# Ten TensorE transposes of an attention and MLP kernel given to the DMA queue, and spatial weights loaded later

## Chip, cores and metric

The kernel runs on one core of a Trainium2 chip. The metric is device time in microseconds (us) of one execution. Before the change the median of three runs is 210.61 us (210.47 to 212.0).

## What is computed

Block-sparse attention over 4 batches of 8 heads, 768 positions, head width 64, and after it a gated MLP with a spatial (position by position) product. Cut to what matters:

```python
scores = q @ k.T / sqrt(D)                   # mask: band, edges, sampled blocks of 32
attn   = exp(scores - max) ; attn /= attn.sum(-1)
x      = (attn @ v), heads side by side      # (4, 768, 512)
h      = relu(x @ w_in)                      # (4, 768, 1024)
u, v   = h[..., :512], h[..., 512:]
v_n    = (v - mean(v)) / sqrt(var(v) + 1e-6)
v_s    = w_spatial @ v_n + b_spatial         # over positions
out    = (u * v_s) @ w_out
```

## The kernel before

**Pairs.** Two heads make a pair; pairs 0 to 3 are batch 0, pairs 4 to 15 the other three. For a pair, q, k and v are loaded as float32 (`st_q`, `st_k`, `st_v`, 384 KB each, `load`, L105) by the SP queue and cast to bfloat16 by GpSimd (`cast`, L117): q and k into `nat`, v into `vv`. TensorE needs q and k with the head dimension on the partitions, in the tile `kq`. For pairs 1 to 3 TensorE transposes them through PSUM and VectorE copies them out (`tr_first`: k and the first third of q; `tr_rest`, L346: the last two thirds of q). From pair 4 on one DMA transpose does a whole pair (`tr_dma`, L365: `nat` to `tt`), and VectorE copies each head out of `tt` into `kq` (`split`, L369).

**Slots.** The work is written out by hand as a list of slots, one after another. Slot s issues the score matmuls of step s into one of two PSUM tiles (tag `sc`), from which ScalarE takes the exponential into `a_all`, then the attention-times-v matmuls (AV) of an earlier step, then whatever `when(slot, ...)` put there, then as many matmuls of the MLP as a pace gives (`run_queue`), and at last what stands in `late[slot]`. Each engine runs its own instructions in this order; an instruction that waits holds all behind it on its engine, and this holds for SP, which issues nearly all DMAs.

**The first 36 slots** are batch 0, in which the mask is applied, so that it goes by units of one third of the queries: `UNITS` (L377) are head 0 and head 1 of pair 0 (two thirds of the queries), then pairs 1, 2, 3 with the first third (units 2, 3, 4), pairs 1, 2, 3 with the second (units 5, 6, 7), and pairs 0 to 3 with the last (units 8 to 11). A unit takes three slots: unit u scores in slots 3u to 3u + 2, and its AV matmuls follow three slots later. So the last third of q of pair 1, 2 and 3 is first wanted in slots 27, 30 and 33. Slot 36 is the first with the unmasked `qk_full` of pair 4, head 0 of `kq`.

**From attention to the MLP.** When a unit's AV is done, VectorE normalizes it into `xn` (L431; tiles `xn3`, three buffers), and `xtr_third` (L491) has TensorE transpose it into the unused end of its own PSUM tile and VectorE copy it into `xt`, one tile per pair, of which the unit fills its third. The MLP of batch 0 runs in steps of one matmul: product v2 (and v3, u2, u3) is dealt out from slot 29 on, and its four matmuls load as weights, in turn, the second third of `xt` of pairs 0, 1, 2, 3. The product's result is taken out of PSUM by VectorE (`vn`, `un`).

**Spatial weights.** `w_spatial` comes in six loads of 384 KB (`ws_load`, L517), each cast by GpSimd in three pieces (`ws_cast`, L522), and each two are transposed by one DMA (`ws_tr`, L530) into `w_spt`, which the spatial products of batch 0 use first.

Of the kernel before, what the change touches and what calls it, by code (L numbers as in the profile page):

```python
# [11 lines left out]
BF16 = mybir.dt.bfloat16  # L12
# [14 lines left out]
def kernel(  # L27
# [16 lines left out]
    nc = tc.nc  # L44

    B, H, S, D = q.shape
# [3 lines left out]
    NCH = S // 128  # L50
# [6 lines left out]
    NG = H // 2  # L57
# [4 lines left out]
    NT = 3  # L62
    TC = NCH // NT
    TW = TC * 128
# [4 lines left out]
    const = ctx.enter_context(tc.tile_pool(name="const", bufs=1))  # L69
# [12 lines left out]
    kq = const.tile([128, H, 2 * S], BF16, name="kq")  # L82
# [6 lines left out]
    def qcols(t0, n=1):  # L89
        return slice(S + t0 * TW, S + (t0 + n) * TW)  # L90
# [20 lines left out]
    nat = {}  # L111
# [97 lines left out]
    def dve_copy(o, i):  # L209
        nc.vector.tensor_copy(out=o, in_=i)  # L210
# [47 lines left out]
    def bank(nm="ps", tag=None):  # L258
        return psum.tile([128, 1024], BF16, tag=tag or moe_tag(), bufs=2 if tag else 1, name=nm)

    def tr(ps, c, in_):
        nc.tensor.transpose(out=ps[:, c * 128:(c + 1) * 128], in_=in_, identity=ident)  # L262

    def pair_of(src, c):
        return src[:, c].rearrange("p h d -> p (h d)")
# [7 lines left out]
    def head(ps, h, c0, n, at=0):  # L273
        for i in range(0, n, 2):
            nc.tensor.transpose(out=ps[:, at + i * 64:at + (i + 2) * 64],
                                in_=nat0_view()[:, h, (c0 + i) * D:(c0 + i + 2) * D],
                                identity=ident)
# [66 lines left out]
            dve_copy(kq[0:D, 2 * p + h, 0:S + TW], ps[h * D:(h + 1) * D, :])  # L344

    def tr_rest(p, t0=1):  # L346
        src = nat[p] if p == 0 else nat.pop(p)
        ps = bank()
        n = NCH - t0 * TC
        if p == 0:  # L350
            for h in range(2):
                head(ps, h, 2 * NCH - 2, 2, h * 128)
            for odd in range(2):
                dve_copy(kq[0:D, 0:2, S + (NCH - 2 + odd) * 128:S + (NCH - 1 + odd) * 128],
                         ps[odd * D:(odd + 1) * D, 0:256].rearrange("d (h n) -> d h n", h=2))
            return
        for c in range(n):
            tr(ps, c, pair_of(src, 2 * NCH - n + c))
        for h in range(2):
            dve_copy(kq[0:D, 2 * p + h, qcols(t0, NT - t0)], ps[h * D:(h + 1) * D, 0:n * 128])  # L360


    tt = {}
# [10 lines left out]
    a_ref, av_ref, x_ref, xn_ref, xt_ref = {}, {}, {}, {}, {}  # L374


    UNITS = [("h", 0), ("h", 1)] + [(0, p) for p in range(1, NG)] + \  # L377
# [101 lines left out]
    def xt_tile(p):  # L479
        if p not in xt_ref:  # L480
            xt_ref[p] = work.tile([128, S], BF16, tag="xt", bufs=7, name="xt")
        return xt_ref[p]

    def xtr_pe(p, xn, c0, n, ps=None):
        if ps is None:
            ps = bank()
        for c in range(n):
            tr(ps, c, pair_of(xn, c))
        dve_copy(xt_tile(p)[:, c0 * 128:(c0 + n) * 128], ps[:, 0:n * 128])

    def xtr_third(u):  # L491
# [4 lines left out]
        else:  # L496
            xtr_pe(p, xn_ref.pop(u), t * TC, TC, x_ref.pop(u))


    def xtr_rest(p):  # L500
        nc.sync.dma_start_transpose(
            out=xt_tile(p)[:, 256:].rearrange("p (c n) -> p c n", c=NCH - 2),
            in_=xn_ref["p", p][:, 2:].rearrange("p c h d -> p (c h d)"))
# [201 lines left out]
    at, late, pre = {}, {}, {}  # L705

    def when(slot, *fns):
        at.setdefault(slot, []).extend(fns)

    def c(f, *a, **kw):  # L710
        return lambda: f(*a, **kw)
# [11 lines left out]
    for p, sl in ((2, 14), (3, 15)):  # L723
        late.setdefault(sl, []).append(c(tr_rest, p))
# [4 lines left out]
    for p, sl in ((1, 11), (0, 18)):  # L729
        when(sl, c(tr_rest, p, 2 if p == 0 else 1))  # L730
    for u, slot in enumerate((13, 14, 15, 19, 22, 25, 28, 30, 34, 37, 40), 1):
        (pre if u == 2 else late).setdefault(slot, []).append(c(xtr_third, u))

    def moe_begin(b):
        moe[b] = Moe(b)
# [56 lines left out]
    def slot_of(p):  # L792
        return S0 + 12 * (p - NG)

    for p in range(NG, NP):
        g = slot_of(p)
        when({4: 14, 5: 20, 6: 28, 11: g - 29, 15: g - 29}.get(p, g - 36), c(load, p, "k"), c(load, p, "q"), c(load, p, "v"))
        when({4: 17, 5: 23, 6: 37, 11: g - 22, 15: g - 22}.get(p, g - 24),
             *[c(cast, p, nm, PL, cs=cs) for nm in "kqv" for cs in (((C01, C23, C45) if p > 5 else (ALLC,)))])
        when({4: 21, 5: 27, 11: g - 18, 15: g - 18, 10: g - 17, 14: g - 17}.get(p, g - 19), c(tr_dma, p))  # L800
        if p % NG == 1 and p > 2 * NG:
            late.setdefault(g - 4, []).append(c(split, p, 0))
        else:
            when(g - 5, c(split, p, 0))
        when(g + 4 if p == NG else g - 3, c(split, p, 1))
        if p == NP - 1:
            when(g + 20, last_x)
        elif p % NG == NG - 1:
            when(g + 19, c(xtr_rest, p))
            late.setdefault(g + 20, []).append(c(xtr_two, p))  # L810
        else:
            when(g + 20, c(xtr_dma, p))
    for i, (ld, ca) in enumerate([(15, 19), (15, 20), (23, 27), (23, 28), (33, 39), (33, 47)]):
        when(ld, c(ws_load, i))
        when(ca, c(ws_cast, i))
    for i, sl in enumerate((24, 30, 50)):
        when(sl, c(ws_tr, i))
    when(50, *[c(w_out_load, g) for g in range(NDH)])
    when(58, *[c(w_out_cast, g, PL) for g in range(NDH)])
# [3 lines left out]
    for u in range(len(UNITS)):  # L823
        for e in range(3):
            sl = (5, 5, 7)[e] if u == 0 else 3 * u + e + (4 if u < 3 else 3)
# [54 lines left out]
```

## Time and profile before

| what | us |
|---|---|
| median of three runs | 210.61 |
| the profiled execution | 211.73 |
| its span, first to last instruction | 209.9 |
| TensorE busy | 201.3 |
| ScalarE busy | 168.8 |
| VectorE busy | 136.4 |
| GpSimd busy | 83.3 |

The granted TensorE clock is 0.996 of full speed over the span. SP's queue moves 41.24 MB in 64228 packets, 76% of the time of the 16 DMA engines; 45716 of all packets are under 512 bytes. Busy time of TensorE counts a matmul from its start to its modelled end, and one starts before the one before it has ended, so a matmul's listed duration is more than it takes of the engine: two 128-column transposes are listed as 0.27 us, and the next matmul starts 0.11 us after the first of them.

The stage that the change touches lies between 12 and 48 us, in slots 11 to 40. In it the TensorE transposes of `nat` are 28 instructions in 128-column pieces from 12.5 to 21.5 us, those of `xn` 24 from 19.4 to 45.8 us. VectorE's copies that belong to them are `kq<-ps` of 64x512 at 0.42 us each (six) and `xt<-ps_av` of 128x256 at 0.28 us (ten). A median 384 KB load takes 4.4 (k), 4.9 (q) or 6.0 us (v) from issue to landing, a DMA transpose 5.7 us (`tt`, 12 blocks of 128x128), 3.1 (`gt`, mostly 8 blocks) and 2.8 (`xt`, 6 or 4 blocks).

### The profile page before, as it was taken

To read this page: it belongs to the slowest core of one execution; us is meant where nothing else is said; L and a number is where in the kernel's file an instruction comes from. 1 tells how busy PE (TensorE), PEld (TensorE's weight loads), DVE (VectorE), ACT (ScalarE), POOL (GpSimd) and SP (SyncE) were. 2 spreads that over 40 slices of the span, in tenths; PEclk is the share of its full clock that TensorE was granted. 3 is DMA by queue.
4 is the path that set the end of the run, shared out by engine and by line. 5 is a ranking of instruction groups with operands and counts; after the bars stand their busy time and mean duration, and the time that the engine had idled before them with its cause. 6 is when DMAs were issued, how large, how long until landed. Compare 5 with 4: busy or idle time off the path is not lost.

```text
span 209.9 us, 5319 instructions
## 1 busy us (share of the span) xinstructions
PE 201.3 (96%) x2106; PEld 129.1 (61%) x2140; DVE 136.4 (65%) x301; ACT 168.8 (80%) x222; POOL 83.3 (40%) x184
## 2 busy tenths in 40 slices
PE   8789999999999999999999999999999999999993
PEld 6569878766666666665566556665566556544441
DVE  7768987999874756484975454284985443476551
ACT  6979999999999999979998888979889787266021
POOL 6689869957828726006159051006220000012000
PEclk9999999999999999999999999999999999999998
DMA  5999799999999999999965497478501225610256
GB/s 162 330 357 344 222 314 285 251 301 359 250 338 188 264 165 296 270 219 345 210 216 112 116 247 179 153 177 262 102 3 35 53 53 116 222 54 0 50 146 228
DMA packets 64684, 41.96 MB, mean 200 GB/s; under 512 B 45716, under 2 KB 59412, under 8 KB 64660
## 3 DMA queue, kind: packets, MB, share of 16 engines
q1 hardware_dynamic: 64228, 41.24, 76.0%
q10 hardware_dynamic: 432, 0.39, 0.6%
q8 instruction: 16, 0.26, 0.5%
q14 instruction: 8, 0.07, 0.1%
HBM read 24.38 MB, written 6.29 MB: 146 GB/s over the span
## 4 chain that ended last, share of the span: by engine, by line
PE 87%; DMA 4%; DVE 2%; SPq 1%; ACT 1%; issue 1%; POOL 0%; ACTq 0%
PE ps_moe L555 31%; PE ps L421 22%; PE ps_av L469 13%; PE ps_t L555 7%; PE ps L408 6%; PE ps_av L451 4%; DMA st_k<-in_k_dram 4%; PE ps_sc L555 3%; PE ps L262 1%; SPq L108 1%; DVE kq L210 1%; ACT a_all L413 1%; DMA out_dram<-osb 1%; PE ps_av L262 1%; ACT osb L213 0%
## 5 line engine op out<-in xcount | busy, mean ns | idle before, releaser
L424 ACT ACTIVATE a_all<-ps 128x768 bf16<-128x768 f32 x144 | 113.7, 811 | 15.5 <-PE ps L421 7.2
L421 PE MATMUL ps<-kq 128*128 128x512 bf16 (+1 forms) x288 | 70.3, 325 | 0.2
L469 PEld LDWEIGHTS <-a_all 128*128 128x128 bf16 x864 | 46.6, 98 | 19.4
L469 PE MATMUL ps_av<-vv,a_all 128*128 128x65 bf16 x864 | 51.0, 194 | 0.1
L421 PEld LDWEIGHTS <-kq 128*128 128x128 bf16 x288 | 27.8, 97 | 30.1 <-issue 0.2
L555 PE MATMUL ps_moe<-w_in_t,xt 128*128 128x512 bf16 x128 | 39.4, 378 | 0.5
L413 ACT ACTIVATE a_all<-ps 128x1024 bf16<-128x1024 f32 x35 | 33.9, 1024 | 1.9 <-PE ps L408 1.4
L136 POOL CAST nat<-st_k 128x256 bf16<-128x256 f32 (+3 forms) x37 | 16.7, 482 | 42.9 <-DMA st_k<-in_k_dram 31.4
L555 PE MATMUL ps_moe<-vn,w_spt 128*128 128x512 bf16 x98 | 30.5, 378 | 0.6
L592 POOL TENSOR_SCALAR std<-mv 128x3 f32<-128x3 f32 (+1 forms) x9 | 2.1, 238 | 50.8 <-DVE mv L589 36.9
L408 PE MATMUL ps<-kq 88*128 88x256 bf16 (+1 forms) x136 | 21.0, 275 | 1.0 <-DVE kq L210 0.6
L623 DVE SCALAR_TENSOR_TENSOR un<-ps_moe,b_col,un 128x512 bf16<-128x512 f32 x18 | 13.5, 748 | 12.9 <-PE ps_moe L555 10.9
L555 PE MATMUL ps_moe<-w_out_t,gt 128*128 128x512 bf16 x66 | 20.2, 378 | 0.1
L555 PEld LDWEIGHTS <-xt 128*128 128x128 bf16 x192 | 15.2, 97 | 7.1 <-DVE xt L210 0.2
L433 DVE RECIPROCAL rc<-ps_av 128x6 f32<-128x6 f32 (+1 forms) x36 | 6.6, 184 | 19.9 <-PE ps_av L469 18.8
L434 DVE TENSOR_TENSOR xn<-ps_av,rc 128x384 bf16<-128x384 f32 (+1 forms) x36 | 18.5, 513 | 1.2
L136 POOL CAST nat<-st_q 128x256 bf16<-128x256 f32 (+2 forms) x41 | 17.2, 447 | 3.9 <-DMA st_q<-in_q_dram 3.6
L136 POOL CAST vv<-st_v 128x256 bf16<-128x256 f32 (+1 forms) x36 | 17.4, 516 | 3.1 <-DMA st_v<-in_v_dram 3.0
L588 DVE BATCH_NORM_STATS2 stats<-vn 128x6 f32<-128x512 bf16 x24 | 16.5, 688 | 1.5 <-ACT vn L583 0.9
L184 DVE TENSOR_SCALAR vn<-ps_moe 128x512 bf16<-128x512 f32 x18 | 12.3, 683 | 6.0 <-PE ps_moe L555 6.0
L451 PE MATMUL ps_av<-vv,a_all 128*128 128x65 bf16 x288 | 14.6, 194 | 1.0 <-POOL vv L136 1.0
L451 PEld LDWEIGHTS <-a_all 128*128 128x128 bf16 x288 | 13.5, 98 | 2.7 <-issue 1.5
(92 smaller groups left out, 215.5 us busy)
## 6 DMA issues: line engine op xcount, KB each, us to landing
st_v<-in_v_dram SPq DMA_DIRECT2D x16, 384.0 KB, 6.0
out_dram<-osb SPq DMA_DIRECT2D x23, 256.0 KB, 2.4
st_k<-in_k_dram SPq DMA_DIRECT2D x15, 384.0 KB, 4.4
st_q<-in_q_dram SPq DMA_DIRECT2D x12, 384.0 KB, 4.9
ws_f<-in_moe_w_spatial_dram SPq DMA_DIRECT2D x6, 384.0 KB, 4.7
w_f<-in_moe_w_in_dram SPq DMA_DIRECT2D x8, 256.0 KB, 5.6
w_f<-in_moe_w_out_dram SPq DMA_DIRECT2D x4, 256.0 KB, 5.6
st_q<-in_q_dram SPq DMA_DIRECT2D x3, 256.0 KB, 6.9
```

The lines of the kernel that those rows point to most:

```text
L136: eng.tensor_copy(out=dst, in_=src)
L184: nc.vector.tensor_scalar(out=out, in0=in0, scalar1=s1, scalar2=s2, op0=o0, **kw)
L408: nc.tensor.matmul(out=ps[:, at:at + n * TW], lhsT=kq[0:KR, h, ci * 128:(ci + 1) * 128], rhs=kq[0:KR, h, qcols(t0, n)], start=True, stop=True)
L413: nc.scalar.activation(out=out, in_=ps, func=AF.Exp, scale=0.125)
L421: nc.tensor.matmul(out=ps[:, n0:n1], lhsT=kq[:, j % H, ci * 128:(ci + 1) * 128], rhs=kq[:, j % H, S + n0:S + n1], start=True, stop=True)
L424: nc.scalar.activation(out=a_ref["h", j][:, ci, :], in_=ps[:, 0:S], func=AF.Exp, scale=0.125)
L434: nc.vector.tensor_tensor(out=out, in0=ps[:, :, 0:D], in1=rc[:, 0:n].to_broadcast([128, n, D]), op=ALU.mult)
L451: nc.tensor.matmul(out=av_ref[u][:, to, :], lhsT=a_ref[u][:, at:at + 128], rhs=vv[pp % NVV][:, h, ci, :], start=(ci == 0), stop=(ci == NCH ...
L469: nc.tensor.matmul(out=av_ref[j][:, qc, :], lhsT=a_ref["h", j][:, ci, qc * 128:(qc + 1) * 128], rhs=vv[p % NVV][:, h, ci, :], start=(ci == ...
L555: nc.tensor.matmul(out=ref["ps"][:, 0:w], lhsT=lhs(i), rhs=rhs(i), start=(i == 0), stop=(i == n - 1))
L588: nc.vector.bn_stats(out=stats, in_=self.vn[:, tcc, :])
L623: nc.vector.scalar_tensor_tensor(out=self.un[:, tcc, :], in0=ps, scalar=b_col[:, tcc:tcc + 1], in1=self.un[:, tcc, :], op0=ALU.add, op1=AL ...
```

## The change

`tr_rest` of pairs 1 to 3 transposes only the second third of q on TensorE. The last third goes by a DMA transpose of two blocks into a new tile `tq` (`trq_dma`, issued late in slot 15 for all three pairs), and VectorE copies it into `kq` head by head (`trq_split`, late in slots 25, 27, 29). The `xt` thirds of units 5 and 6 (pairs 1 and 2, second third) go from `xn` to `xt` by a DMA transpose of two blocks each (`xtr_third_dma`, late in slots 20 and 23), in place of TensorE and the VectorE copy in slots 22 and 25.

The first two loads of `w_spatial` move from slot 15 to slot 22, the next two stay in slot 23; the casts of these four move from slots 19, 20, 27, 28 to 26, 27, 28, 29, and the first two spatial transposes from slots 24 and 30 to 29 and 32. The transpose `tr_dma` of pair 4 moves from slot 21 to slot 24. In the built program SP's order from pair 4's loads on is: three `tq`, pair 5's loads, `xt` of unit 5, four spatial loads, `xt` of unit 6, `tt` of pair 4, `tt` of pair 5, pair 6's loads, two `w_spt`. Before it was: two spatial loads, pair 5's loads, `tt` of pair 4, two spatial loads, the first `w_spt`, `tt` of pair 5, pair 6's loads, the second `w_spt`.

```diff
     def tr_rest(p, t0=1):
-        src = nat[p] if p == 0 else nat.pop(p)
+        src = nat[p]
...
-        for c in range(n):
-            tr(ps, c, pair_of(src, 2 * NCH - n + c))
+        for c in range(TC):
+            tr(ps, c, pair_of(src, NCH + t0 * TC + c))
         for h in range(2):
-            dve_copy(kq[0:D, 2 * p + h, qcols(t0, NT - t0)], ps[h * D:(h + 1) * D, 0:n * 128])
+            dve_copy(kq[0:D, 2 * p + h, qcols(t0)], ps[h * D:(h + 1) * D, 0:TW])
+
+    tq = const.tile([128, NG, TC, 128], BF16)
+
+    def trq_dma(p):
+        nc.sync.dma_start_transpose(
+            out=tq[:, p], in_=nat.pop(p)[:, 2 * NCH - TC:].rearrange("p c h d -> p (c h d)"))
+
+    def trq_split(p):
+        for h in range(2):
+            dve_copy(kq[0:D, 2 * p + h, qcols(2)],
+                     tq[h * D:(h + 1) * D, p].rearrange("d c n -> d (c n)"))
...
+    def xtr_third_dma(u):
+        t, p = UNITS[u]
+        x_ref.pop(u)
+        nc.sync.dma_start_transpose(
+            out=xt_tile(p)[:, t * TW:(t + 1) * TW].rearrange("p (c n) -> p c n", c=TC),
+            in_=xn_ref.pop(u).rearrange("p c h d -> p (c h d)"))
...
     for u, slot in enumerate((13, 14, 15, 19, 22, 25, 28, 30, 34, 37, 40), 1):
-        (pre if u == 2 else late).setdefault(slot, []).append(c(xtr_third, u))
+        if u not in (5, 6):
+            (pre if u == 2 else late).setdefault(slot, []).append(c(xtr_third, u))
+    for u, slot in ((5, 20), (6, 23)):
+        late.setdefault(slot, []).append(c(xtr_third_dma, u))
+    for p, slot in ((1, 25), (2, 27), (3, 29)):
+        late.setdefault(15, []).append(c(trq_dma, p))
+        late.setdefault(slot, []).append(c(trq_split, p))
...
-        when({4: 21, 5: 27, 11: g - 18, 15: g - 18, 10: g - 17, 14: g - 17}.get(p, g - 19), c(tr_dma, p))
+        when({4: 24, 5: 27, 11: g - 18, 15: g - 18, 10: g - 17, 14: g - 17}.get(p, g - 19), c(tr_dma, p))
...
-    for i, (ld, ca) in enumerate([(15, 19), (15, 20), (23, 27), (23, 28), (33, 39), (33, 47)]):
+    for i, (ld, ca) in enumerate([(22, 26), (22, 27), (23, 28), (23, 29), (33, 39), (33, 47)]):
         when(ld, c(ws_load, i))
         when(ca, c(ws_cast, i))
-    for i, sl in enumerate((24, 30, 50)):
+    for i, sl in enumerate((29, 32, 50)):
         when(sl, c(ws_tr, i))
```

## The prediction

> **What bounds the kernel.** I read the page's engine row first, then the chain of waits between 12 and 46 us, where everything that the change touches lies.
>
> ```profile
> PE 201.3 (96%) x2106; PEld 129.1 (61%) x2140; DVE 136.4 (65%) x301; ACT 168.8 (80%) x222; POOL 83.3 (40%) x184
> ```
> ```profile
> 36.45 0.21 PE ps_moe L555
> 36.67 0.11 PE ps_av L262 x2
> 36.78 0.44 PE ps L408 x4
> 37.22 0.26 PE ps_av L451 x8
> 37.48 0.43 PE ps_moe L555 x2
> ```
>
> Columns of the chain: start, length, engine and line. Each piece begins where the one before ends, and so it goes from about 16 us until the tail: TensorE is fed without a hole. The few gaps of 0.2 us, about one in 4 to 5 us, are each just one 512-column matmul long and stand where one is due, so I take them for missing records. Two transposes are 0.11 us, one matmul of the MLP 0.215 us, a slot of this stage about 0.98 us. So whatever TensorE is spared, it gains, and whatever it waits, it loses.
>
> The Trainium skill ("Perfetto Trace Analysis", Identifying the Most-Contended Engine) calls matmul busy time a poor measure and goes by weight loads; by that, 61% busy (81% between 25 and 35 us), TensorE would have room, and sparing it would be worth 0 instead of the 0.55 us below. The unbroken chain decides here against that.
>
> Next, what feeds this stage: SP's queue, the DMA rate, and VectorE around the place where the new transfers are used.
>
> ```profile
> 23.86 0.47 SPq L108 DMA_DIRECT2D st_v<-in_v_dram  x1
> 24.37 0.94 SPq L519 DMA_DIRECT2D ws_f<-in_moe_w_spatial_dram  x2
> 25.36 1.18 SPq L108 DMA_DIRECT2D st_k<-in_k_dram  x1
> 26.58 0.94 SPq L108 DMA_DIRECT2D st_q<-in_q_dram  x1
> 27.57 0.95 SPq L108 DMA_DIRECT2D st_v<-in_v_dram  x1
> 29.65 4.33 SPq L367 DMA_TRANSPOSE tt<-nat  x1
> 34.02 1.04 SPq L519 DMA_DIRECT2D ws_f<-in_moe_w_spatial_dram  x2
> ```
> ```profile
> 25.00:30.00 5.00, 4.95 (x71) 4.03 (x71) 4.14 (x12) 4.69 (x6) 3.13 (x5) 1.00 0.95 297
> 30.00:35.00 5.00, 4.95 (x71) 4.04 (x71) 4.03 (x11) 4.95 (x6) 4.69 (x9) 1.00 1.21 325
> ```
> ```profile
> 38.07 0.28 DVE L210 COPY xt<-ps_av 128x256 bf16<-128x256 bf16 x1
> 38.27 0.85 DVE L210 COPY kq<-tt 64x1536 bf16<-64x1536 bf16 x1
> 39.05 0.73 DVE L184 TENSOR_SCALAR vn<-vn,mv,rstd 128x512 bf16<-128x512 bf16 x1
> 39.71 0.17 DVE L433 RECIPROCAL rc<-ps_av 128x4 f32<-128x4 f32 x1
> 39.91 0.42 DVE L434 TENSOR_TENSOR xn<-ps_av,rc 128x256 bf16<-128x256 f32 x1
> ```
>
> The last two columns of the middle table are the DMA engines' share and GB/s: they are full. Issue to landing, asked one by one: pair 4's v 6.0 us (lands 29.9), the first two spatial loads 6.5 (the first lands 30.9), pair 5's v 8.1 (35.7), pair 4's transpose `tt` 7.4 (37.0), the next two spatial loads 4.0 and 4.4 (38.0, 39.0). They land in the order of issue, one 384 KB load per 1.0 to 1.2 us: one queue, with several loads of backlog. VectorE reaches the copy out of `tt` at 38.27, 1.2 us after the landing, and goes on with no hole; its `xn` of unit 9 ends at 40.33, and TensorE transposes it at 40.48. So VectorE has 0.1 us of slack there, and the `tt` transfer 1.2.
>
> **What is removed.** Ten TensorE transposes: two for each of pairs 1, 2, 3 (slots 11, 14, 15) and two each for units 5 and 6 (slots 22, 25). 5 x 0.11 = 0.55 us, all on the path. ScalarE can follow: its exps take 1.02 us each and start 0.92 us apart when nothing delays them, against slots of 0.98. VectorE: six 64x512 copies of 0.42 become six 64x256 from PSUM at 0.295 (the 0.59 us pair at 25.07) and six from `tq` in SBUF. Such a copy is not in the trace; the 64x1536 SBUF copy takes 0.52 to 0.85, a sixth of it is 0.09 to 0.14, the PSUM row 0.295 is the upper end; I take 0.2. With two `xt` copies of 0.28 gone VectorE's work is the same within 0.2 us (2.5 + 0.56 out, 1.8 + 1.2 in). Before 37 us it waits for TensorE at each normalization (0.40 us at 35.58), which hides it; without that cover it would cost those 0.2 us.
>
> **What is added on SP and DMA.** Five transposes of two blocks (64 KB). For SP the nearest rows are the shortest transposes: 4 blocks 1.19 to 1.23 us, 6 blocks 1.2 to 2.1. Five are 6 us of SP. From 24.37: three `tq` 3.6, pair 5's loads 3.1, `xt` of unit 5 1.2, four spatial loads 2 (at 0.5) to 4 (at 1.0), `xt` of unit 6 1.2: issued by 35.5 to 37.5, and a transpose that finds no backlog lands 1.5 us after its issue ends (88.44: issue 1.23, landing 2.7), so 37.0 to 39.0. SP alone is no later than what follows.
>
> For DMA time: a 6-block transpose landed 0.6 us after the one before it (74.15 + 3.7 behind 71.58 + 5.7) and 0.7 (63.80 + 4.0 behind 60.49 + 6.6), `tt` 1.3 us after pair 5's v for 12 blocks: 0.11 us a block. `w_spt` (35.16 + 6.5 behind 39.0) gives 0.22. Ten blocks cost 1.1 us (to 2.2); I take 1.1, since three rows agree.
>
> **What is moved.** Spatial loads 0 to 3 go from ahead of (and behind) `tt` to a place where all four stand ahead of the transpose of unit 6's `xt`, and `tt` of pair 4 stands behind that. So ahead of `tt` now come two loads more (1.0 us each, 38.0 and 39.0) and five small transposes (1.1): 37.05 + 2.0 + 1.1 = 40.15 us. Unit 6's `xt` lands 1.3 before, at 38.85.
>
> Who waits? (a) TensorE: the third matmul of product v2, in slot 31, loads weights from pair 2's `xt`, columns of third 1, which unit 6 makes. It ran at about 37.54 (the second of the two from 37.32); 0.55 us earlier now, 37.0. It waits 1.85 us, with the exps' matmuls queued behind it. Unit 5's lands at about 34.5, the three `tq` at 30.1 to 30.8, both ahead of need (36.8; the copies stand behind the memset of 31.3). (b) VectorE stops at the copy of `tt` from 38 until 40.2, and queued behind it are the scaling of `vn`, the normalization of unit 9 and, at 41.79, the `xt` copy that frees a PSUM tile for the AV matmuls of slot 36. These end 40.2 - 38.27 = 1.9 us later than before, so TensorE's transposes of unit 9, at 40.48 before, come at 42.4. That is measured against before, so it holds the 0.55 us already: both stalls are pinned to a landing, and the later one, (b), decides. TensorE has no hole later to win it back.
>
> The rest costs nothing: the `w_spt` transposes landed at 41.7 and 48.5, the first is used at 55.4 and the second some ten us later; moved behind pair 6's loads they land around 47 to 49. If that cover went, each us would be one of TensorE. GpSimd's twelve casts (0.64 each) now follow pair 5's casts in one run and end about 44; the `std` behind them ran at 44.23 for a `vn` at 47.4, two us of slack. Pair 5's loads land a little earlier without two spatial loads ahead; its `tt` likewise.
>
> **Sum.** -0.55 if nothing waits; with (b), +1.9. The profiled execution took 211.73 us (span 209.9); 213.6. The median is 210.61, 1.1 lower; I add to it: 212.5.
>
> **Rivals.** *The DMA queue keeps up* (faster end). A landing is that of the last of 16 engines; the others may be ahead of it. From 24.4 us, when pair 4's loads begin, 4.65 MB have to pass up to the end of `tt` (ten loads of 0.39 MB, 0.33 in small transposes, 0.39). At the 357 to 361 GB/s that the queue moved from 10 to 20 us that is 12.9 to 13.0 us, so 37.4 plus up to 1 for the landing: no wait for `tt`, 0.3 or none for `xt`. Then 210.05, up to 210.9 with small waits. Against it: 297 and 325 GB/s in this very stretch, and small packets. It decides if `tt` lands before 38.4. *Small transposes are dear*: each added one holds the stream as `w_spt` did (0.22 a block) and costs up to 0.3 more in issue, so `tt` at 41.3 to 42.8, +3.0 to +4.5, 213.6 to 215.1. The 1.9 to 2.9 us that some 12-block transposes took to land after the transfer ahead speak for it, the 0.6 us rows against.
>
> The Trainium skill ("DMA: Bandwidth & Descriptors", Rules for kernel authors) says that transfers under 64 KB pay mostly overhead and names some 2 us of fixed cost; five such in series would be 10 us and 221 us in all. By that rule; the trace disagrees: transposes overlap in the queue, 0.6 us apart.
>
> **Numbers.** About 1% (2.1 us) is what can be told from no change. Forecast, waits of 1 to 3.5 us in all: 0.68, its range 211.1 to 213.6 (210.61 - 0.55 + the wait). Queue keeps up: 0.20 (210.05 to 211.1). Dear transposes: 0.12. The boundary, 212.7, is at `tt` = 40.35, a hair above my landing, so the forecast's chance is halved there: slower 0.34 + 0.12 = 0.46, same 0.34 + 0.16 = 0.50, faster 0.04: no case here gives 2.1 us, and this is for what I don't see. Range: 210.5, inside the fast case, to 214.2, inside the dear one.
>
> **What will show it.** TensorE's wait for `xt` from the DMA in slot 31 of about 1.9 us; VectorE's wait for `tt` at about 38; `tt` landing near 40; a hole in the chain between 36 and 43 us and none after. No such hole, and 0.55 us less, would prove the fast rival; a hole at the `tq` copies, or at `w_spt` after 55 us, would mean that I misplaced the late transfer.

## The result and the profile after

The changed kernel takes 216.67 us, median of six runs (215.45 to 218.35); the kernel before, run beside it, takes 211.84 (210.47 to 213.25, six runs). The ratio is 1.0252, 95% interval 1.0213 to 1.0291: 5.3 us slower, where 1.9 were forecast. The profiled execution took 216.86 us, its span is 215.1; before it was 211.73 and 209.9.

The engine row and the clock row of the page (one digit for each fortieth of the span, 9 is full speed):

```profile
PE 205.9 (96%) x2130; PEld 130.6 (61%) x2130; DVE 137.9 (64%) x305; ACT 168.5 (78%) x222; POOL 83.6 (39%) x184
...
PEclk9999999679999999999999999999999999999999
```

TensorE has ten transposes less to do and is busy 4.6 us longer. The clock row says why: in the eighth and ninth fortieth, 37.6 to 48.4 us, it ran below full speed. The chain of waits through that stretch (start, length, what):

```profile
33.75 5.76 DMA xt<-xn
39.51 0.05 issue
39.56 0.61 PE ps_moe L573
40.17 0.85 PE ps L419 x4
...
41.46 0.43 PE ps_moe L573
```

The unbroken chain of before now has a DMA in it, the transpose of unit 6's `xt`, issued at 33.75 and landing at 39.51. What follows is slow: four score matmuls were 0.44 us of the chain, they are 0.85; one MLP matmul was 0.21, it is 0.43. TensorE's own timeline gives the length of the wait in brackets, and the windows (the columns after the five engines are the clock and the DMA engines' share) how long the clock stayed down:

```profile
35.75 0.38 PE L573 MATMUL ps_moe<-w_in_t,xt 128*128 128x512 bf16 x1
39.56 0.61 PE L573 MATMUL ps_moe<-w_in_t,xt 128*128 128x512 bf16 x1 [3.43 <-DMA xt<-xn]
```
```profile
30.00:35.00 5.00, 4.93 (x70) 3.75 (x67) 4.61 (x13) 4.97 (x6) 4.45 (x7) 1.00 1.04 343
35.00:40.00 5.00, 1.57 (x18) 0.94 (x18) 3.11 (x6) 1.45 (x2) 5.00 (x9) 0.88 1.13 288
40.00:45.00 5.00, 5.00 (x40) 3.54 (x39) 3.18 (x7) 2.55 (x3) 3.70 (x6) 0.50 1.00 264
```

The clock is at half speed, 0.50, from 38.83 to 45.65 us (by the trace's clock record; the 0.88 of 35 to 40 us is the first 1.2 us of it), though TensorE has work again from 39.56. All six executions show it: four have a granted clock of 0.984 over the span and took 216.5 to 218.4 us, two have 0.992, half the loss, and took 215.5 and 215.6. The Trainium skill ("TensorE: Matmul & The Clock Gate", Part 1: The HAM clock gate) says that the array drops to half its clock after an idle window of some 3.4 us and needs as long a busy one to return. In the trace the clock fell when TensorE had been idle for 2.70 us, so less was enough here, and it came back 6.1 us after the work did.

SP's order and VectorE's wait, the other two views of before:

```profile
31.59 2.07 SPq L537 DMA_DIRECT2D ws_f<-in_moe_w_spatial_dram  x4
33.75 1.17 SPq L514 DMA_TRANSPOSE xt<-xn  x1
35.02 5.56 SPq L378 DMA_TRANSPOSE tt<-nat  x2
```
```profile
38.09 0.28 DVE L210 COPY xt<-ps_av 128x256 bf16<-128x256 bf16 x1
40.84 0.55 DVE L210 COPY kq<-tt 64x1536 bf16<-64x1536 bf16 x1 [2.48 <-DMA tt<-nat]
```

SP issued the transpose of unit 6 by 34.9 us; it landed 4.6 us later, behind four spatial loads that landed at 35.2, 36.2, 38.1 and 39.2. Pair 4's `tt` landed at 40.8.

**Where the 5 us are.** TensorE's first MLP matmul starts at 22.38 before and 20.89 after, 1.49 earlier: six transposes less are 0.33 of it, most of the rest is one hole of 1.0 us that the profiled run of before had at 10 us while waiting for the first cast of v. From there to the matmul that needs unit 6's `xt` it was 15.16 us (to 37.54) and would have been 15.08 (to 35.97). The hole ahead of it is 3.59 us. (A hole is counted here from when the next matmul was due. That is 0.16 us more than the wait in brackets, which starts at the listed end of the matmul ahead; further down a hole is placed by the start of that matmul.) From it to the first matmul of slot 36 it was 4.17 us (37.54 to 41.71) and is 7.06 (39.56 to 46.62): 2.89, of which the clock has the most. -1.49 - 0.08 + 3.59 + 2.89 = 4.91, and slot 36 starts 4.91 us later. From there to the last matmul nothing changes by more than 0.1 us.

### The profile page after: what moved, and what is told of

Same layout as the page of the kernel before. It is cut to its first block, busy times and chain, and to the rows that moved or that the text cites. A ratio compares the mean times of both kernels' runs of the same rounds, so it can differ in the third digit from the quotient of the medians.

```text
span 215.1 us, 5344 instructions
## 1 busy us (share of the span) xinstructions
PE 205.9 (96%) x2130; PEld 130.6 (61%) x2130; DVE 137.9 (64%) x305; ACT 168.5 (78%) x222; POOL 83.6 (39%) x184
## 4 chain that ended last, share of the span: by engine, by line
PE 86%; ACT 5%; DMA 4%; DVE 3%; issue 0%; ACTq 0%
PE ps_moe L573 32%; PE ps L432 22%; PE ps_av L480 13%; PE ps_t L573 6%; PE ps L419 4%; ACT a_all L424 3%; PE ps_sc L573 3%; PE ps_av L462 3%; DMA xt<-xn 3%; PE wps L178 1%; DMA out_dram<-osb 1%; PE ps L262 1%; DVE kq L210 1%; DVE kq L746 1%; ACT a_all L414 1%; ACT osb L213 0%
## 5 line engine op out<-in xcount | busy, mean ns | idle before, releaser
L432 PE MATMUL ps<-kq 128*128 128x512 bf16 (+1 forms) x288 | 70.3, 325 | 0.0
L480 PEld LDWEIGHTS <-a_all 128*128 128x128 bf16 x864 | 46.6, 98 | 19.4
L480 PE MATMUL ps_av<-vv,a_all 128*128 128x65 bf16 x864 | 51.0, 194 | 0.0
L573 PE MATMUL ps_moe<-w_in_t,xt 128*128 128x512 bf16 x144 | 44.9, 384 | 3.4 <-DMA xt<-xn 3.4
L432 PEld LDWEIGHTS <-kq 128*128 128x128 bf16 x288 | 27.8, 97 | 30.1 <-issue 0.2
L424 ACT ACTIVATE a_all<-ps 128x1024 bf16<-128x1024 f32 x35 | 33.7, 1025 | 6.7 <-PE ps L419 6.6
L573 PE MATMUL ps_moe<-vn,w_spt 128*128 128x512 bf16 x108 | 32.7, 378 | 0.0
L419 PE MATMUL ps<-kq 88*128 88x256 bf16 (+1 forms) x136 | 22.6, 290 | 0.7 <-DVE kq L210 0.6
L573 PE MATMUL ps_moe<-w_out_t,gt 128*128 128x512 bf16 x72 | 21.5, 378 | 0.0
L136 POOL CAST nat<-st_q 128x256 bf16<-128x256 f32 (+2 forms) x41 | 18.2, 471 | 2.3 <-DMA st_q<-in_q_dram 2.2
L419 PEld LDWEIGHTS <-kq 88*128 88x128 bf16 x136 | 13.1, 102 | 5.2 <-issue 1.2
L210 DVE COPY kq<-tt 64x1536 bf16<-64x1536 bf16 x24 | 14.2, 594 | 2.8 <-DMA tt<-nat 2.5
```

The lines of the kernel that those rows point to most:

```text
L136: eng.tensor_copy(out=dst, in_=src)
L419: nc.tensor.matmul(out=ps[:, at:at + n * TW], lhsT=kq[0:KR, h, ci * 128:(ci + 1) * 128], rhs=kq[0:KR, h, qcols(t0, n)], start=True, stop=True)
L424: nc.scalar.activation(out=out, in_=ps, func=AF.Exp, scale=0.125)
L432: nc.tensor.matmul(out=ps[:, n0:n1], lhsT=kq[:, j % H, ci * 128:(ci + 1) * 128], rhs=kq[:, j % H, S + n0:S + n1], start=True, stop=True)
L480: nc.tensor.matmul(out=av_ref[j][:, qc, :], lhsT=a_ref["h", j][:, ci, qc * 128:(qc + 1) * 128], rhs=vv[p % NVV][:, h, ci, :], start=(ci == ...
L573: nc.tensor.matmul(out=ref["ps"][:, 0:w], lhsT=lhs(i), rhs=rhs(i), start=(i == 0), stop=(i == n - 1))
```

## The experiments

Theory when they were planned: the DMA queue delivers unit 6's `xt` and pair 4's `tt` too late (A), and the clock that falls in the wait doubles the price. Rivals: the holes have different causes (B: with the one gone, the other holds); the small transposes cost on their own, wherever they stand (C). Later ones are in the expectations.

**Unit 6's x back on TensorE.**

```diff
-        if u not in (5, 6):
+        if u != 5:
-    for u, slot in ((5, 20), (6, 23)):
+    for u, slot in ((5, 20),):
```

> Theory A (the place of unit 6's xt transfer behind four spatial loads makes TensorE wait, and the wait is long enough that the clock falls after it): with unit 6's x back on TensorE the wait of 3.4 us and the slow clock are gone. If that were all, 0.45 us under the kernel before, ratio 0.998. Theory B (pair 4's tt, late for VectorE, holds TensorE too, only hidden behind the longer wait): tt lands near 40.6, VectorE waits about 2.5 us for it, TensorE shows a hole of 2 to 2.7 us ahead of unit 9's transposes, too short for the clock to fall, ratio 1.007 to 1.011. Theory C (the two-block DMA transposes are dear in themselves): four of five are left, ratio 1.02.

The profiled execution took 214.35 us at a clock of 0.996. The three others took 218.7 to 219.3 at 0.984, the lower clock of the changed kernel's executions; there is no trace of them, so where they lost it is not known, the time of this version stays open, and what follows holds for the profiled execution alone. The waits of TensorE in the profile (us in total, times, longest), and VectorE's timeline:

```profile
PE ps_av L462 <- DVE xt L210: 1.6, 2, 1.0
PE ps_av L262 <- DVE xn L445: 1.5, 1, 1.5
```
```profile
32.79 1.62 DVE L210 COPY kq<-tq 64x256 bf16<-64x256 bf16 x2
```

The wait for unit 6 is gone, 1.15, 0.74 and 1.69 us of other holes stand at 34.4, 38.7 and 40.7 us, and the clock held in this execution. VectorE waits 0.99 us for `tt`, and the hole of 1.69 us stands behind that: so the late `tt` costs time too (B), though less than the 2 to 2.7 us expected. And VectorE is late in a way that no theory had named: two `tq` copies of 64x256 take 1.62 us. GpSimd's casts of pair 4 lie beside them: `nat` is cast from 29.26 on, after a wait of 4.03 us that ends as the first `tq` transpose lands, because pair 4 is cast into the buffer that this transpose reads. Before, that cast stood at 26.85.

**The wait filled.** Sixty matmuls of 128 columns, whose result is not used, run in slot 31 ahead of the one that waits.

```diff
+    when(31, lambda: filler(60, psum.tile([128, 1024], FP32, tag="sc", bufs=2, name="fs")))
```

> 60 matmuls of 128 columns (3.3 us) whose result nobody reads stand in slot 31 just ahead of the matmul that waits for unit 6's xt. Theory A: they fill the wait, the clock stays at 1.0, the wait left over is under 0.5 us, and the time falls by what the slow clock costs, about 2.5 us: ratio 1.011 to 1.015 instead of 1.025. If the slow stretch after the wait is not due to TensorE standing idle, the clock still falls between 39 and 46 us and the ratio stays at 1.023 or more.

1.0227 (1.0151 to 1.0304), so the time expected, 1.011 to 1.015, was missed; 216.13 us profiled, clock 1.000. TensorE around the filler, and where slot 36 begins (L432):

```profile
37.47 3.51 PE L178 MATMUL fs<-warm 128*128 128x128 bf16 x60
41.03 0.38 PE L573 MATMUL ps_moe<-w_in_t,xt 128*128 128x512 bf16 x1
...
45.76 0.49 PE L432 MATMUL ps<-kq 128*128 128x512 bf16 x2
```

With TensorE kept at work the matmuls behind are at full speed, and the way to slot 36 is 4.73 us (41.03 to 45.76) in place of 7.06: the clock is worth 2.3 us, and its fall comes of the idle time. The time of the kernel hardly shows it: unit 6 landed at 39.9, 0.4 us later than in the changed kernel, and the filler, which began 1.0 us late behind a late VectorE copy at 35 us, ended 1.1 us after that landing.

**The spatial loads behind pair 4's `tt`**, all five DMA transposes kept:

```diff
-[(22, 26), (22, 27), (23, 28), (23, 29), (33, 39), (33, 47)]
+[(25, 30), (25, 31), (26, 32), (26, 33), (33, 39), (33, 47)]
-enumerate((29, 32, 50))
+enumerate((31, 34, 50))
```

> All five DMA transposes stay; the four spatial loads are issued behind pair 4's tt instead of ahead of unit 6's xt. Theories A and B: xt of unit 6 lands near 34.5 to 35, tt of pair 4 near 36 to 37, no wait on TensorE or VectorE for either, clock 1.0, and the 0.55 us of removed transposes show: ratio 0.995 to 0.999. Theory C: the transposes are still there, ratio over 1.01.

1.0053 (1.0022 to 1.0084). Unit 6 lands at 36.0 and `tt` at 37.1, nothing waits for either, and the clock stays: 4.2 us of the 5.3 come back with four loads moved. That is the place in the queue, and the strong form of (C) falls. But 0.995 to 0.999 was expected. What is left are holes of 0.48 and 0.46 us:

```profile
32.23 0.61 PE L419 MATMUL ps<-kq 88*128 88x256 bf16 x4 [0.32 <-DVE kq L210]
36.21 0.42 PE L462 MATMUL ps_av<-vv,a_all 128*128 128x65 bf16 x8 [0.30 <-DVE xt L210]
```

They are VectorE's lateness again, with `tq` copies of 0.21 to 0.76 us beside GpSimd's late cast. The profiled execution lost 0.9 us more between 80 and 110 us, in holes of under 0.5 us each.

**The moves alone**: the changed order of loads and `tt`, all transposes on TensorE (the diff of the change without its transposes).

> Only the moves (spatial loads, their casts and transposes, tt of pair 4 to slot 24), all ten transposes on TensorE. Theory B: tt lands 39 to 39.5, VectorE waits about 1 us for it, ratio 1.003 to 1.007. Theory C, and theory A without B: ratio 1.000.

1.0016 (0.9986 to 1.0046). `tt` lands at 38.06, VectorE waits 0.9 us for it, TensorE has one hole of 1.03 us at 39.1. The moves are not the 5 us; they take the slack that the transposes then lack.

**As two runs above, with a fifth buffer for `nat`** (and one less for the staged spatial loads, for room).

```diff
-tag="nat", bufs=4
+tag="nat", bufs=5
-tag="ws_f", bufs=6
+tag="ws_f", bufs=5
```

> As the run with the four spatial loads behind tt, with a fifth buffer for nat (and five instead of six for the spatial loads, to make room). Theory D, formed after that run: GpSimd's cast of pair 4 takes over pair 1's nat buffer, and has to wait for tq of pair 1 (29.5 us) where before TensorE had read it by 21.5; the late casts then run beside VectorE's copies out of tq, which grow from 0.2 to as much as 0.85 us each. With the fifth buffer the cast of pair 4 runs from about 27, the tq copies take 0.2 to 0.3, the holes of 0.48 and 0.46 us near 31.5 and 35.6 are gone: ratio 0.996 to 0.999. If the tq copies are slow in themselves, the holes stay and so does 1.005.

1.0057 (1.003 to 1.0085). Pair 4's cast starts at 26.95, all six `tq` copies take 0.21 or 0.22 us, and both holes are gone: that reading was right, but the time expected with it, 0.996 to 0.999, did not come. A new one of 1.44 us stands at 34.4:

```profile
36.03 0.28 PE L262 MATMUL ps_av<-ident,xn 128*128 128x128 bf16 x2 [1.27 <-DVE xn L445]
```
```profile
35.55 0.42 DVE L445 TENSOR_TENSOR xn<-ps_av,rc 128x256 bf16<-128x256 f32 x1 [1.70 <-DMA xt<-xn]
```

VectorE's normalization of unit 8 writes the third buffer over, that of unit 5, which the DMA transpose still reads. TensorE's transposes read such a tile within some 0.3 us (that of unit 9, before, was written by 40.33 and read from 40.48 on); the DMA lets go of it when it has landed, at 35.4.

**Two of the four spatial loads behind `tt`.**

```diff
-[(22, 26), (22, 27), (23, 28), (23, 29), (33, 39), (33, 47)]
+[(22, 26), (22, 27), (25, 30), (25, 31), (33, 39), (33, 47)]
```

> Two of the four spatial loads ahead of unit 6's xt, two behind pair 4's tt. Theory A: xt of unit 6 lands two loads earlier, at about 37.5, the wait in slot 31 is about 1.5 us and too short for the clock to fall, tt lands near 38.8: ratio 1.008 to 1.013, so under half of what the whole change costs for half of the loads, since the clock's 2.3 us go as well. If the cost is simply proportional to the loads ahead: 1.015.

1.0074 (1.0042 to 1.0105), in reach of theory A's 1.008 to 1.013; 1.015 is out. Unit 6 lands at 38.45. Two short holes, 0.97 us for the reused buffer and 1.23 for the transfer, and yet, in the profiled execution:

```profile
36.35 0.60 PE L419 MATMUL ps<-kq 88*128 88x256 bf16 x4
...
38.50 0.61 PE L573 MATMUL ps_moe<-w_in_t,xt 128*128 128x512 bf16 x1 [1.07 <-DMA xt<-xn]
38.90 1.06 PE L419 MATMUL ps<-kq 88*128 88x256 bf16 x4
```

The four score matmuls are 0.60 before the second hole and 1.06 after it: half speed, from 38.44 to 41.85 us. So two holes close together are enough, where a single one of 1.69 us was not. This was the longest of ten executions, with a clock of 0.991; eight of them have 0.995 or more, so the ratio is mainly that of executions in which the clock held.

**Only units 5 and 6 by DMA**, loads as in the third run, no `tq`.

> Units 5 and 6 by DMA, the last thirds of q back on TensorE, spatial loads behind tt. Theory D: nothing waits for tq, GpSimd casts pair 4 at about 27, no hole: 0.22 us are left of the gain, ratio 0.997 to 1.001. Theory C (small transposes dear): two are left, 1.002 or more with waits at the xt transfers.

1.0083 (1.0042 to 1.0125), runs of 212.1 to 216.8. Until 83 us TensorE has no hole, and from its first MLP matmul to its first spatial product it takes 32.81 us (21.11 to 53.92) against 33.09 (22.38 to 55.47): 0.28 less, where four transposes at 0.055 are 0.22. Then:

```profile
86.11 0.39 PE L573 MATMUL ps_moe<-w_out_t,gt 128*128 128x512 bf16 x1 [2.73 <-DMA gt<-un]
86.56 0.84 PE L432 MATMUL ps<-kq 128*128 128x512 bf16 x2
```

The transposed gate input lands at 86.1, behind the loads of pair 10 (its v at 83.6). TensorE waits, and its clock is halved from 86.53 to 89.95. No theory had a wait at that place. In the profile of before the same transpose landed at 83.67 for a matmul at 84.8. This execution was 1.55 us ahead of that one by then (1.27 of it from the start), and met a queue that runs 5 to 7 us from issue to landing there. It is one of the slower executions (215.21, clock 0.991); nine of the twelve have a clock of 0.996 or more, so what the others lost is not shown by it.

**Only `tq`**, spatial loads and `tt` as before the change.

> The kernel before with only the last thirds of q by DMA, spatial loads and tt where they were. Theory D: GpSimd's cast of pair 4 waits for tq and ends near 31 to 32 instead of 30.7, tt of pair 4 is issued after it and with 0.9 us more ahead lands near 38.5 to 40; VectorE has slow tq copies and then waits for tt: holes of 1 to 2.5 us, ratio 1.004 to 1.012. Without theory D: tt at 37.9, ratio 0.998.

1.0159 (1.0086 to 1.0231). Behind two spatial loads the three land at 32.6 to 33.7, VectorE waits 1.19 us for the first, and slot 27 for the copy:

```profile
32.86 0.61 PE L419 MATMUL ps<-kq 88*128 88x256 bf16 x4 [1.11 <-DVE kq L210]
```

So with those two loads ahead `tq` comes too late, and moving them had its reason. The ratio is not shown by this trace: the profiled execution is the shortest of four (213.33, clock 0.998), and the others took 214.9 to 217.0 at 0.991 or 0.992. Pair 4's cast, at 26.84, does not wait for a transpose here; why the buffer is another one in this program was not followed up.

**Both buffers more**, on the third run's order and on the change's own.

```diff
-tag="xn3", bufs=3
+tag="xn3", bufs=4
```

> All five DMA transposes, the four spatial loads behind the transpose of pair 4 as in the earlier run, five nat buffers, and a fourth buffer for the normalised query thirds, so that unit 8's does not wait for the transpose of unit 5. Theory E (the late landings, the cast of pair 4 behind the last-third transposes and the reuse of unit 5's buffer are all that the change costs): no hole of TensorE over 0.3 us between 20 and 50 us, last-third copies of 0.21 to 0.22 us, clock 0.99 or more, time 0.996 to 1.000 of before. Theory F (what is gained ahead of 50 us is given back around 80 us, where the transposed gate input landed 83.67 in the profile of before, about 1 us ahead of the matmul that reads it, behind loads that are 5 us behind): a wait of TensorE for gt around 83 us as in the run with the x transposes alone (2.7 us there), and 1.000 to 1.008. The last-third transposes themselves cost time on the queue (theory C): VectorE waits for xt or tq by DMA of 0.3 us or more remain, 1.002 to 1.006.

> The changed kernel with five nat buffers and a fourth buffer for the normalised query thirds; all issues and spatial loads stand where the change has them. Theory E (the queue order is the main cause, the buffers only a later one): the transpose of unit 6 still lands at 38.5 to 40 us, TensorE waits 3 to 3.7 us for it and its clock falls for about 5 us, 1.018 to 1.026 of before. Rival (the buffers hold back the queue, so that the transposes come late because of them): the cast of pair 4 starts at about 27 us, its transpose lands before 39 us, the wait for unit 6 is below 2 us, the clock stays, and the time is 1.003 to 1.012.

The first took 1.0075 (1.0044 to 1.0106), where theory E had 0.996 to 1.000. The cast and buffer waits are gone, but 0.61 us at 35.5 (unit 6 lands at 36.3), 1.60 at 45.2 and 1.03 at 85.0 stand in their place. The second of them is a wait for this copy of VectorE, beside these casts of GpSimd:

```profile
44.30 2.67 DVE L210 COPY kq<-tt 64x1536 bf16<-64x1536 bf16 x1
```
```profile
39.49 7.07 POOL L546 CAST ws_b<-ws_f 128x256 bf16<-128x256 f32 x12 [3.54 <-DMA ws_f<-in_moe_w_spatial_dram]
```

By its place, in slot 40, it is the copy of head 1 out of pair 4's `tt`, which had landed at 37.4; slot 42 needs that head. It took 2.67 us, where the other twelve profiles have 0.56 to 1.02, and ended 0.42 us after the last of the twelve spatial casts, which GpSimd runs without a pause from 39.5 on, after a wait for their loads. So the hole is not due to the landing of pair 5's `tt` (45.3), as the next expectation assumes. The third is a wait for the gate's transpose again. The second took 1.0268 (1.0231 to 1.0306): with the order of the change the buffers win nothing, unit 6 lands at 40.5 and TensorE waits 4.06 us. Order first, buffers second, as theory E said of that run, with a little more of both than it had.

**Three more issues spread out**: two spatial loads behind pair 5's `tt`, the second spatial transpose four slots later, pair 10's loads behind the gate's transpose.

```diff
-[(25, 30), (25, 31), (26, 32), (26, 33), (33, 39), (33, 47)]
+[(25, 30), (25, 31), (27, 35), (27, 36), (33, 39), (33, 47)]
-enumerate((31, 34, 50))
+enumerate((31, 38, 50))
-11: g - 29, 15: g - 29}.get(p, g - 36)
+10: g - 30, 11: g - 29, 15: g - 29}.get(p, g - 36)
```

> As the run with five nat and four query-third buffers, with three issues moved: two of the four spatial loads behind the transpose of pair 5 (its late landing, 45.3 us, held TensorE 1.6 us there), the second spatial transpose behind the loads of pair 7, and the loads of pair 10 behind the gate's transpose and pair 9's (TensorE waited 1.0 us for gt at 85 us). Theory E (each wait has one cause and goes with it): pair 5's transpose lands before 43.5 us, no hole of TensorE over 0.4 us between 20 and 110 us, and 0.995 to 1.000 of before. Theory F (the DMA engines have work without a gap from 22 to 90 us, and 2 to 3 us of transposes more come out as a wait at one place or another): a hole of over 0.5 us somewhere in that stretch, and 1.001 to 1.007.

1.0131 (1.0083 to 1.0179), the worst of the repairs. From 18 to 80 us TensorE has no hole above 0.15 us, as theory E wanted, though pair 5's `tt` landed only at 44.9. What this edit parts is the run of spatial casts (a pause from 44.5 to 45.9 us), and the copy of head 1 took 0.72 us. Between 80 and 110 us three of 0.36, 0.33 and 0.47 stand. These do not make 2.8 us. The profiled execution (215.32, the longest of six) also lost time at a place that no edit touches: the same work at 12 us runs at half speed in it,

```profile
11.97 1.06 PE L419 MATMUL ps<-kq 88*128 88x512 bf16 x2
```

where the run with both buffers has 0.59 us at 9.93. Its TensorE came to full speed at 13.8 us; in the profiles of the other kernels that was between 3.6 and 6.3. By 18 us it was 1.7 us behind the profile of before, where the other changed ones were 0.2 to 1.5 ahead. Whether the other five runs of this kernel began so is not known, and its time stays partly unexplained.

No version beat the kernel before; the moves alone are equal to it, every version with a DMA transpose whose ratio is known is 0.5% slower or more.

**What the five transposes take of the queue.** From the landing of pair 4's v to that of pair 5's `tt`, the same nine large transfers pass in nine of the runs:

| run | v of pair 4 lands | `tt` of pair 5 lands | between | small transposes |
|---|---|---|---|---|
| moves alone | 28.02 | 41.00 | 12.98 | 0 |
| units 5 and 6 only | 29.50 | 43.47 | 13.97 | 2 |
| unit 6 on TensorE | 28.70 | 43.22 | 14.52 | 4 |
| the wait filled | 29.14 | 43.80 | 14.66 | 5 |
| the change | 28.27 | 43.82 | 15.55 | 5 |
| the change, more buffers | 29.72 | 44.95 | 15.23 | 5 |
| two loads behind `tt` | 29.76 | 44.88 | 15.12 | 5 |
| loads behind `tt` | 29.18 | 45.10 | 15.92 | 5 |
| the same, fifth `nat` buffer | 28.90 | 44.47 | 15.57 | 5 |

Against the one run without any, two add 1.0 us, four 1.5, five 1.7 to 2.9: 0.3 to 0.6 us for each of 64 KB, 0.2 to 0.3 a block. (The run with both buffers and the loads behind has 17.40, with pauses of 1 to 2 us inside single loads.)

## The prediction, step by step

- **TensorE is fed without a hole, so it gains what it is spared.** Right, and the run with units 5 and 6 alone measured it, in one profile against one: 0.28 us for four transposes against 0.22.
- **SP is no later than the DMA engines.** Right: the small transposes took 1.17 to 1.27 us of issue here, 1.2 was taken, and unit 6's was issued by 34.9.
- **DMA time of ten blocks, 1.1 us (to 2.2).** Too small: 2.6 in the changed kernel, 1.7 to 2.9 in all runs with five. The rows of 0.6 us between 6-block transposes were taken over the one row of 0.22 a block; the latter was the nearer one. By the interval since pair 4's v, unit 6's landing was forecast 9.0 us behind it (38.85 after 29.89) and came 11.2 behind (39.51 after 28.27).
- **(a) TensorE waits for unit 6 in slot 31, 1.85 us.** The mechanism, the matmul and the place are right; the wait is 3.43. The absolute landing was only 0.7 us later than forecast; the need was 1.0 us earlier (35.97 for 37.0), since the profiled run of before had begun late: none of the other twelve profiles has its hole of 1.0 us at 10 us.
- **(b) decides: VectorE's wait for `tt`.** VectorE did stop, at 38.4, for 2.48 us, landing 40.8 for 40.15. But TensorE was held by (a) by then, and behind it ran so slowly that the copies were in time. (a) decided. With the clock kept up, in the filled run, the way to slot 36 was still 4.73 us for 4.17, so (b) is worth some 0.6.
- **No step for the clock.** This is the step that failed the sum: the wait was priced at its own length. The clock fell in it, and that cost 2.3 us by the filled run, up to 2.9 with what (b) adds. A wait of 1.85 us as forecast would have stood at the edge: 1.82 us without a matmul within 3.41 halved the clock in one run, 1.54 did not in another (last section).
- **`tq` copies at 0.2 us, VectorE's work the same.** Right at 0.21 to 0.26 when no cast of GpSimd held them, up to 0.88 when one did. No hole of the changed kernel hangs on it; in three repaired ones 0.3 to 1.0 us do.
- **Buffers.** The prediction let TensorE's transposes go as work and did not ask when the DMA that replaces them lets go of what it reads. `nat` and the `xn3` of unit 5 are held some 4 us and more, issue and queue included. This cost nothing in the changed kernel, whose larger wait covered it, and 1 to 1.4 us in the repaired ones.
- **`w_spt` and GpSimd's spatial casts cost nothing.** Right here: the two `w_spt` land at 48.4 and 50.4, the spatial product starts at 60.3. In the run with both buffers the casts did cost: the hole of 1.60 us.
- **A hole between 36 and 43 us and none after.** Right.
- **The rivals.** That the queue keeps up is out. Dear transposes, 0.22 a block, were nearly right for the DMA's part and not for the time, since they too had no step for the clock. Nor did five transposes cost 10 us of queue: 1.7 to 2.9.
- **The profile set 1.1 us above the median.** The median of three, 210.61, was low: beside the changed kernel the one of before is 211.84, the profile's 211.73. Taking 1.1 off made the forecast lower than its own sum of 213.6.

By the two profiled executions, from the sixteenth microsecond on: 0.3 to 0.4 us gained, 3.59 lost in the hole, 2.89 behind it, 6.2 us in all, of which the earlier start of the one execution hides 1.2 to 1.5; the medians have 4.8, the ratio 5.3. Of the 3.4 us that the forecast is short, the clock is 2.3. The remaining 1.1 are argued and not measured: the wait was 1.6 us longer than forecast, and the start of the two profiled executions differs by about as much.

## What to carry to other kernels

Giving a transpose to a DMA queue that is full trades 0.055 us of TensorE for 0.2 to 0.3 us of queue per block, and every later transfer in that queue pays; look for the ones with the least slack, all the way down the kernel, since a repair at one of them moves the wait to the next. Where a bound TensorE may be made to wait, add up its holes over 3.4 us: at 1.8 us or more, price the matmuls behind them at half speed for 3 to 6 us as well. And when a DMA takes over reading a tile, its buffer is held until the landing: ask who writes there next.

## What was not expected of the hardware

- The clock changes in steps. Counted from its first rise to full speed, every change in the thirteen profiles before the last matmul lies on a multiple of 3.41 us; half speed lasted 6.83 us in the changed kernel and 3.41 in three others. It fell at the end of a step in which TensorE had no matmul, by the listed ends, for 1.82 us (two of the loads behind `tt`: two holes together), 2.69 (the change), 2.77 (units 5 and 6 only) or 3.41 (the change with more buffers). It held after every other step from there on, the idlest with 1.54 us. So the sum of the holes in one step counts here, and where a hole lies between two steps as well as its length. Behind the fall the changed kernel still had 0.73 us without a matmul in the next step, and a second one at half speed followed; that this is the reason rests on the one case. Keeping TensorE at work with matmuls of no use kept the clock up.
- How long TensorE begins at half speed differs between executions that start with the same code: full speed came at 3.6 to 6.3 us, in one profile at 13.8.
- VectorE's 64x256 copies out of `tq` took 0.21 to 0.26 us, or 0.44 to 0.88 beside a GpSimd cast. All 26 long ones of the 60 in these profiles end 0.07 to 0.09 us after the end of a cast that was running when they began. So such a copy is not slowed by the cast, it is held until the cast is over. Beside GpSimd's small `std` and `rstd` operations copies took 0.21 to 0.26 us.
